# Gated linear attention and a sticky top-1 MoE on one core: next states scaled on ScalarE, and matmuls of zeros moved inside the output product

## The chip, the cores and the metric

The kernel runs on one core of a Trainium2 chip. Times are device microseconds of one execution; the number that counts is the median over the timed runs. Engines are named as in the profile: PE (matrix products), DVE (VectorE), ACT (ScalarE), POOL (GpSimd), SP (SyncE, which here only issues DMAs). PEld is PE's loading of weights.

## The reference, cut to what matters

Four sequences, eight heads, 768 tokens, head dimension 48. Each head keeps a 48x48 state that decays per row and takes in k times v; then each token of 384 numbers goes to one of eight experts:

```python
for t in range(S):
    state = alpha[:, :, t, :, None] * state + np.einsum('bhd,bhe->bhde', k[:, :, t], v[:, :, t])
    y[:, :, t] = np.einsum('bhd,bhde->bhe', q[:, :, t], state)
...
fresh_e = int(np.argmax(logits[b, s]))
e = fresh_e if s == 0 or local_gate[b, s] < 0.5 else prev_e
h = np.maximum(x[b, s] @ w1[e], 0.0)        # 384 -> 1024
out[b, s] = p[e] * (h @ w2[e])              # 1024 -> 384, p: softmax of the logits
```

A token may keep the expert of the token before it (`prev_e`), so the choice runs in order through each sequence.

## The kernel before, in words

**Blocks.** The attention is done in 24 blocks of 128 tokens (two chunks of 64, `C`): block i is chunk pair i // 4 of sequence i % 4, so four blocks, a group, advance all four sequences by 128 tokens, and the state that block i leaves is the start of block i + 4. Four heads lie beside each other twice (partitions 0 to 47 and 64 to 111). The pieces of a block, with the lines of the functions:

- `load_a`, `load_x`, `load_v` (299 to 313): SP issues the loads of decays, of k and q, and of v. `first_v` (315) copies the first 64 rows of v on ACT, beside a half of zeros, so that one product can serve both chunks.
- `scan1` (319): DVE runs products of the decays (`A`) and their reciprocal, POOL scales q by `A`. `scan2` (336): DVE runs the backward scan `sf`, POOL scales k. `one_a` (332): a small POOL memset in the decays that these scans need.
- `kt` (344): PE transposes k into the PSUM tile `kp`, ACT copies it out as `kk`.
- `pm` (353): PE makes the products of k and q (`pe`), DVE masks them into `pq`.
- `um` (369): PE makes the updates `up` from `kk` and v; DVE adds them to the start state and so makes `st`.
- `copies` (390): two ACT copies bring `st` into the operand `sb`. `state` (395): DVE scales the end state by the decay of the block and writes it as the start of block i + 4.
- `ym` (403): PE makes y into one PSUM tile, first the products of `pq` with v (the value products, 32 in the trace), then those of q with `sb` (the state products, 16). ACT copies y out as `XR` and issues the DMA of `XR` to DRAM (`xd`).
- `xt` (421): PE transposes `XR` into `xp`, ACT copies that to `xx` for the router.

PSUM tiles have one buffer for each tag. `kp` and `xp` have the same tag, `tr`: `xp` of block i - 2 comes after `kp` of block i and is written only when `kk` of block i has been copied out.

**The order.** The engines take their instructions in the order in which the program writes them (`pinned`, line 660 on). In pass i of the loop: `scan2(i+1)`, `kt(i)`, `copies(i-1)`, `state(i-1)`, `pm(i)`, other, `scan1(i+2)`, loads of block i + 3, `xt(i-2)`, `ym(i-1)`, `first_v(i+1)`, a weight step in passes 5 to 11, other, `um(i)`, other.

**Other** (622) fills in work that isn't the block's. It takes one step of the routing generator of a group (`route`, 432: about three steps a block, each up to its next `yield`). Then, until group 2 has been routed, it issues two matmuls of zeros (`dense(DN)`, 293: 128x256, into a tile `h2` that nobody reads). After that it takes pieces of the first expert jobs (`early`, 562: gather rows, transpose them, eight gemm1 steps of nine products, gemm2) for the rows that groups 0 to 2 have given to experts 0 and 1. Expert products are fp32 split in two parts: the high half is cast by ACT, the low half is a difference on DVE, and three products replace one. **A weight step** makes the halves of a slice of expert 0's weights: ACT casts at once, and the low half is put off (`later`, 288) until the next other, that is, ahead of `um` and so ahead of `st` on DVE.

After block 23 and the last routing, the remaining jobs run one after the other, PE full.

Every instruction goes through a helper on line 81, so the profile shows L81 for all of them, and tiles tell them apart. The lines that set the two orders that the change touches:

```python
            if i < NB:
                kt(i)
            if 0 < i <= NB:
                copies(i - 1)
                state(i - 1)
```

Of the kernel before, what the change touches and what calls it, by code (L numbers as in the profile page):

```python
# [42 lines left out]
EARLY = (0, 1)  # L43
NEXT = 2

DN0 = 32
DN = 2
HL = ("h", "h", "up", "pe")
YL = ("yp", "y")
RT = "rt"  # L50
# [16 lines left out]
def gla_moe(ctx, tc, akq, vw, vn, wg, w1, w2, cst, tok, out):  # L67
# [45 lines left out]
    def cc(k, p0=0, p1=128):  # L113
        a, b = _off[k]
        return cs[p0:p1, a:b]
# [140 lines left out]
    with ExitStack() as ac, ExitStack() as aa:  # L256
# [15 lines left out]
            VTs.append(vt)  # L272
        for j in range(2):
            sb = ap.tile([R, 2, 2, CW], F32, bufs=1, name=f"sb{j}")
            g_.memset(sb[0:64], 0.0)
            g_.memset(sb[64:112, :, 1, :], 0.0)
            SBs.append(sb)
            oh = ap.tile([128, E, G + 1], F32, bufs=1, name=f"oh{j}")
            g_.memset(oh, 0.0)
            OHs.append(oh)  # L280

        st = {"c": c0}
        sts = [ap.tile([R, 3, HP, D], F32, tag="st", bufs=G + 1, name=f"st_{i}") for i in range(G)]
# [9 lines left out]
        def dense(n):  # L293
            for _ in range(n):
                t_.matmul(h2[:, 0, 0:C1], lhsT=dz[:, 0:128], rhs=dz[:, 0:C1], start=True, stop=True)
# [15 lines left out]
        def load_v(i):  # L311
            at = i % G * NBB + i // G
            y_.dma_start(VTs[i % NP][:, 1, :], vn[:, at * DM:(at + 1) * DM])

        def first_v(i):
            vt = VTs[i % NP]
            s_.copy(vt[0:64, 0, :], vt[0:64, 1, :])

        def scan1(i):

            d = blk[i]
            x, a = d["x"], d["a"]
            A = ap.tile([R, SW], F32, tag="A", bufs=3, name=f"A_{i}")
            v_.tensor_tensor_scan(A, a[:, 0:SW], z1, 0.0, ALU.mult, ALU.add)
            d["end"] = A[:, 2 * C + 1:SW:2 * (C + 1)]
            v_.reciprocal(z2[0:R, 2 * C + 1:SW:2 * (C + 1)], d["end"])
            q2 = x[:, BW:].rearrange("p (s t) -> p s t", t=C)
            g_.tensor_tensor(q2, q2, A.rearrange("p (s t) -> p s t", t=C + 1)[:, :, 1:], ALU.mult)
            d["k"] = x[:, 0:BW].rearrange("p (h t) -> p h t", h=HP)
            d["q"] = x[:, BW:2 * BW].rearrange("p (h t) -> p h t", h=HP)  # L330

        def one_a(i):
            a = blk[i]["a"]
# [61 lines left out]
        def state(i):  # L395
            d = blk[i]
            if i + G < NB:
                sn = ap.tile([R, 3, HP, D], F32, tag="st", bufs=G + 1, name=f"st_{i + G}")
                v_.scalar_tensor_tensor(sn[:, 0], d["s3"][:, 2], 1.0 / SEED,
                                        d["end"].unsqueeze(2).broadcast_to([R, HP, D]), ALU.mult, ALU.mult)  # L400
                st["S", i % G] = sn

        def ym(i):
            d = blk[i]
            vt, pq = d["vt"][:, 1, :], d["pq"]
            sb = d["sb"].rearrange("p c e (h d) -> p c e h d", h=HP)
            yw = pp.tile([128, 512], F32, tag="y", name=f"y_{i}")
            for h in range(H):
                for c in range(2):
                    r = slice(c * C, (c + 1) * C)  # L410
                    t_.matmul(yw[r, h * D:(h + 1) * D], lhsT=pq[r, h % 2, h // 2, :], rhs=vt[r, h * D:(h + 1) * D],
                              start=(h == 0), stop=False, skip_group_check=True)
            for hp in range(HP):
                for c in range(2):
                    t_.matmul(yw[c * C:(c + 1) * C, 2 * hp * D:2 * (hp + 1) * D], lhsT=d["q"][:, hp, c * C:(c + 1) * C],
                              rhs=sb[:, c, :, hp, :], start=False, stop=(hp == HP - 1), skip_group_check=True)
            d["XR"] = ap.tile([128, DM], F32, tag="XR", bufs=3, name=f"XR_{i}")
            s_.copy(d["XR"], yw[:, 0:DM])
            a_.dma_start(xd[1 + i * 128:1 + (i + 1) * 128], d["XR"])
# [12 lines left out]
        def route(g):  # L432
# [4 lines left out]
            def rt(shape, nm, dt=F32, bufs=2):  # L437
                return ap.tile(shape, dt, tag=nm, bufs=bufs, name=f"{nm}_{g}")
# [27 lines left out]
            v_.scalar_tensor_tensor(m2, kr[:, 1, :, 0], 16.0, m2, ALU.mult, ALU.add)  # L466
            v_.tensor_tensor(kr[:, 0], ge, m2.unsqueeze(2).broadcast_to([128, n, 8]), ALU.is_equal)
            yield
            yield

            rp = pp.tile([8 * n, 2, 128], F32, tag=RT, name=f"rp_{g}")
            for j in range(2):
# [23 lines left out]
            v_.tensor_reduce(se, ex, AX.X, ALU.add)  # L496
            v_.tensor_scalar_add(se, se, 1e-9)
            v_.reciprocal(se, se)
            yield
            v_.tensor_tensor(ex, ex, ob, ALU.mult)  # L500
            pn = rt([128, n], "pn")
            v_.tensor_reduce(pn, ex, AX.X, ALU.add)
            v_.tensor_tensor(pl[:, :, 0], pn, se, ALU.mult)
            yield
            pw = pp.tile([128, E, n + 1], F32, tag=RT, name=f"pw_{g}")
            t_.matmul(pw.rearrange("p e b -> p (e b)"), lhsT=one, rhs=oi.rearrange("p e b -> p (e b)"),
                      start=True, stop=False)
            t_.matmul(pw[:, :, 0:n], lhsT=trif, rhs=o4, start=False, stop=True)
            yield
            ps = rt([128, E, n + 1], "ps")  # L510
            v_.tensor_tensor(ps, pw, st["c"].unsqueeze(2).broadcast_to([128, E, n + 1]), ALU.add)
            po = rt([128, n, 8], "po")
# [20 lines left out]
            (v_ if end else g_).tensor_tensor(vo, oa.unsqueeze(2).broadcast_to([128, n, 3, E * NS]),  # L533
                                              pl.unsqueeze(3).broadcast_to([128, n, 3, E * NS]), ALU.mult)
            on = ap.tile([128, n, TS], F32, bufs=1, tag="on", name=f"on_{g}")
            if end:
                v_.tensor_tensor(on, iob.unsqueeze(1).broadcast_to([128, n, TS]),
                                 rr.unsqueeze(2).broadcast_to([128, n, TS]), ALU.is_equal)
            else:
                for j in range(n):  # L540
                    s_.activation(on[:, j], iob, AF.Abs, bias=rr[:, j:j + 1], scale=-1.0)
                    s_.activation(on[:, j], on[:, j], AF.Relu, bias=one[:, 0:1], scale=-float(TS))
                    if j < n - 1:
                        yield
            yield

            lp = pp.tile([128, 3 * E * NS], F32, tag=RT, name=f"lp_{g}")
# [14 lines left out]
        def early():  # L562
# [7 lines left out]
                j.load_list(0)  # L570
            for _ in jobs[0].gather():
                yield False
            for _ in range(4):
                yield False
            for _ in jobs[0].trans():
                yield True
            for n, j in enumerate(jobs):
# [41 lines left out]

        last, EW, steps = [], {}, []  # L620

        def other(pieces=True):

            flush()
            for r in list(steps):
                if next(r, 0) == 0:
                    steps.remove(r)
            if work[0] is None:
                if DN:
                    dense(DN)  # L630
            else:
                if last and drained[0]:
                    last[0].ht, last[0].yt = HL, YL
                for done in work[0] if pieces else ():
                    if done or steps or not drained[0]:
                        break

        work, drained = [None], [False]
        for i in range(3):
# [3 lines left out]
            if i == 0:  # L643
                nc.scalar.dma_start(cs, cst)
                nc.scalar.dma_start(tk, tok)
                nc.scalar.dma_start(wgs, wg[:, :, 0:32])
        g_.memset(one, 1.0)
        g_.memset(m5, 1.0)
        g_.memset(m5[:, :, 0], 0.0)
        for e in range(E):  # L650
            g_.memset(c0[:, e:e + 1], float(e * RS - 1))
            g_.memset(c1[:, e:e + 1], float(e * RS - 1 + (C1 if e in EARLY else 0)))
        g_.tensor_copy(trif, cc("tri"))
        g_.memset(trif[0:64, 64:128], 1.0)
        g_.memset(trif[64:128, 0:64], 0.0)
        nc.scalar.dma_start(xd[0:1], z2[127:128, 0:DM])
        first_v(0)
        pinned[0] = True
        dense(DN0)
        made = [  # L660
            lambda: g_.memset(fill, 0.0),
            lambda: g_.tensor_copy(fill.bitcast(I32)[:, 1:2], tk[0:SL, 2 * NB:]),
            lambda: g_.memset(acc, 0.0),
# [10 lines left out]
                                     tk[:, 0:2 * NB].rearrange("p (b j t) -> p t j b", b=G, t=2)[:, 0],  # L674
                                     -float(SENT), None, ALU.add),
            lambda: g_.tensor_copy(vals[:, :, 2], tk[:, 1:2 * NB:2]),
        ]
        one_a(0)
        scan1(0)
        scan2(0)  # L680
        one_a(1)
        scan1(1)
        wsteps = iter(())
        for i in range(NB + 2):
            if i + 2 < NB:
                one_a(i + 2)
            if i + 1 < NB:
                scan2(i + 1)
            flush()
            if i < NB:  # L690
                kt(i)
            if 0 < i <= NB:
                copies(i - 1)
                state(i - 1)
            if i < NB:
                pm(i)
            if i > NB:
                drained[0] = True
            for _ in range(min(3, len(made))):
                made.pop(0)()  # L700
            other(i >= NB)
            if i + 2 < NB:
                scan1(i + 2)
            if i + 3 < NB:
                load_a(i + 3)
                load_x(i + 3)
            if i > 1:
                xt(i - 2)
                if (i - 1) % G == 0:
                    steps.append(route((i - 2) // G))  # L710
            if 0 < i <= NB:
                ym(i - 1)
                if i + 2 < NB:
                    load_v(i + 2)
            if i + 1 < NB:
                first_v(i + 1)
            if i == W0:
                begin(EARLY[0], v_)
                wsteps = EW[EARLY[0]].steps()
            elif i > W0 + 2:  # L720
                next(wsteps, None)
            if i == T1:
                begin(EARLY[1], v_)
            other()
            if i < NB:
                um(i)
            other()
# [213 lines left out]
```

## Time and profile before

| what | value |
| --- | --- |
| median of 3 runs | 488.33 us (485.93 to 488.93) |
| profiled execution | 484.0 us, span 482.2 us |
| PE busy | 437.9 us (91%) |
| DVE busy | 257.3 us (53%) |
| ACT busy | 194.1 us (40%) |
| POOL busy | 186.7 us (39%) |
| mean granted clock | 0.961 |
| matmuls of zeros | 142, 35.0 us |
| blocks (first scan to the last `st`) | 6.34 to 169.10 us |

The shares are means over three stages. Up to about 150 us the blocks run and DVE is nearly always busy; from there to 201 us the last blocks, the last routing and the first expert share the engines; from 260 to 470 us PE is busy all the time with expert products (210.00 of 210.00 us). In a row of the order of time stand start and length, engine, line, operation, output and inputs with shapes, the number of merged instructions, and in brackets how long the engine had been idle and what ended that. The start of one `st` and the next gives a block's time.

### The profile page before, as it was taken

To read this page: it belongs to the slowest core of one execution; us is meant where nothing else is said; L and a number is where in the kernel's file an instruction comes from. 1 tells how busy PE (TensorE), PEld (TensorE's weight loads), DVE (VectorE), ACT (ScalarE), POOL (GpSimd) and SP (SyncE) were. 2 spreads that over 40 slices of the span, in tenths; PEclk is the share of its full clock that TensorE was granted. 3 is DMA by queue.
4 is the path that set the end of the run, shared out by engine and by line. 5 is a ranking of instruction groups with operands and counts; after the bars stand their busy time and mean duration, and the time that the engine had idled before them with its cause. 6 is when DMAs were issued, how large, how long until landed. Compare 5 with 4: busy or idle time off the path is not lost.

```text
span 482.2 us, 10873 instructions
## 1 busy us (share of the span) xinstructions
PE 437.9 (91%) x4443; PEld 391.5 (81%) x4443; DVE 257.3 (53%) x485; ACT 194.1 (40%) x390; POOL 186.7 (39%) x207
## 2 busy tenths in 40 slices
PE   5999898999997978698989999999999999999990
PEld 5777776878875877597878998998989989989990
DVE  4778999898997235722274445244254252342310
ACT  1345656565756436321354324335144233242210
POOL 6654326364556000261053642724732503504201
PEclk9799999999998899888899999999999999999997
DMA  8789767596661102660075554444351542531100
GB/s 217 199 260 252 222 187 201 164 292 167 189 208 50 51 17 71 180 186 27 1 224 188 134 181 138 124 131 123 114 175 57 158 130 65 174 98 39 50 3 27
DMA packets 26710, 66.01 MB, mean 137 GB/s; under 512 B 4384, under 2 KB 10677, under 8 KB 26658
## 3 DMA queue, kind: packets, MB, share of 16 engines
q1 hardware_dynamic: 18672, 49.65, 36.3%
q0 software_dynamic: 3840, 10.62, 6.9%
q10 hardware_dynamic: 4146, 5.03, 3.1%
q8 instruction: 35, 0.57, 0.5%
q14 instruction: 17, 0.14, 0.1%
HBM read 55.84 MB, written 10.62 MB: 138 GB/s over the span
## 4 chain that ended last, share of the span: by engine, by line
PE 53%; issue 11%; DVE 9%; ACT 3%; POOL 2%; POOLq 0%; DVEq 0%; ACTq 0%
PE h L81 24%; PE yp L81 20%; PE y L81 3%; PE tp L81 2%; DVE A L81 2%; POOL out L81 1%; PE up L81 1%; DVE st L81 1%; DVE sf L81 1%; DVE pq L81 1%; ACT hh L81 1%; POOL w1l_0b L81 1%; PE pe L81 1%; DVE xl L81 1%; PE lp L81 1%
## 5 line engine op out<-in xcount | busy, mean ns | idle before, releaser
L81 DVE SCALAR_TENSOR_TENSOR hl<-h,hh 128x480 fp32r<-128x480 f32 (+2 forms) x80 | 43.9, 556 | 77.2 <-ACT hh L81 76.9
L81 ACT ACTIVATE hh<-h 128x480 fp32r<-128x480 f32 (+2 forms) x80 | 38.7, 490 | 82.4 <-PE h L81 82.3
L81 POOL DMA_INDIRECT out<-yo,idx x32 | 32.5, 1017 | 80.5 <-DVE yo L81 78.0
L81 POOL DMA_INDIRECT xg<-xd,idx x32 | 32.6, 1018 | 61.0 <-PE tp L81 52.9
L81 DVE TENSOR_SCALAR yo<-yp,acc 128x384 f32<-128x384 f32 (+1 forms) x32 | 19.6, 616 | 61.1 <-PE yp L81 61.0
L81 POOL TENSOR_TENSOR x<-x,sf 112x512 f32<-112x512 f32 x24 | 29.0, 1209 | 42.5 <-DVE sf L81 42.5
L81 POOL TENSOR_TENSOR x<-x,A 112x512 f32<-112x512 f32 x24 | 31.8, 1327 | 29.0 <-DVE A L81 6.6
L81 DVE TENSOR_TENSOR_SCAN A<-a,z 112x520 f32<-112x520 f32 x24 | 34.5, 1437 | 5.6 <-POOL a L81 5.6
L81 PE MATMUL h<-dz 128*128 128x256 f32 x142 | 35.0, 354 | 2.1 <-DVE z L81 2.1
L81 DVE TENSOR_TENSOR_SCAN sf<-a,z 112x520 f32<-112x520 f32 x24 | 33.8, 1408 | 0.1
L81 ACT COPY sb<-st 48x384 f32<-48x384 f32 x48 | 24.5, 510 | 11.5 <-DVE st L81 10.9
L81 PEld LDWEIGHTS h<-dz 128*128 128x128 f32 x142 | 23.8, 224 | 6.5 <-DVE z L81 2.1
L81 PEld LDWEIGHTS y<-vt,pq 64*64 64x64 f32 x768 | 24.9, 138 | 4.0 <-issue 3.8
L81 PE MATMUL y<-vt,pq 64*64 64x48 f32 x768 | 27.9, 224 | 0.0
L81 PE MATMUL y<-sb,x 112*64 112x96 f32 x384 | 21.8, 258 | 4.3 <-ACT sb L81 4.2
L81 PE MATMUL up<-vt,kk 128*48 128x96 f32 (+1 forms) x384 | 23.1, 267 | 0.0
L81 PEld LDWEIGHTS y<-sb,x 112*64 112x64 f32 x384 | 17.2, 140 | 6.2 <-ACT sb L81 5.2
L81 PEld LDWEIGHTS up<-vt,kk 128*48 128x48 f32 (+1 forms) x384 | 18.3, 140 | 3.4 <-issue 1.0
L81 ACT COPY kk<-kp 128x448 f32<-128x448 f32 x24 | 12.8, 531 | 20.7 <-PE kp L81 20.6
L81 PE MATMUL h<-xh,w1h_1a 128*128 128x256 f32 (+1 forms) x48 | 16.4, 342 | 3.9 <-DVE hl L81 2.7
L81 ACT COPY XR<-y 128x384 f32<-128x384 f32 x24 | 11.5, 479 | 20.1 <-PE y L81 20.1
L81 ACT CAST xh<-tp 128x384 fp32r<-128x384 f32 (+1 forms) x32 | 14.0, 462 | 13.9 <-PE tp L81 13.6
(247 smaller groups left out, 1234.8 us busy)
## 6 DMA issues: line engine op xcount, KB each, us to landing
x<-akq SPq DMA_DIRECT2D x24, 448.0 KB, 5.6
a<-akq SPq DMA_DIRECT2D x24, 227.9 KB, 4.5
vt<-vn SPq DMA_DIRECT2D x24, 192.0 KB, 2.7
xd<-XR ACTq DMA_DIRECT2D x24, 192.0 KB, 4.8
rw_0a<-w SPq DMA_DIRECT2D x3, 512.0 KB, 4.9
rw_0a<-w SPq DMA_DIRECT2D x4, 384.0 KB, 4.2
rw_1a<-w SPq DMA_DIRECT2D x3, 512.0 KB, 5.9
rw_1a<-w SPq DMA_DIRECT2D x4, 384.0 KB, 3.5
```

The source lines that it names most:

```text
L81: r = f(*a, **k)
```

## The change

1. `DN` goes from 2 to 0: the six matmuls of zeros of each block go. `DY` = 3 of them are put into `ym`, between the value and the state products, until group 2 has been routed. The 32 at the start stay.
2. `state`: the multiplication on DVE becomes four ACT activations (112x48, a scale for each partition) for every block up to 19; the scale `dec` is made by a small POOL operation in `scan1`.
3. `kt(i)` comes after `copies(i-1)` and `state(i-1)`.
4. `first_v` goes; a second DMA on SP brings the 64 rows.
5. In block 0 the scaling of q comes after that of k on POOL. Memsets of POOL from the start go into the list `made`, which is worked off five at a time instead of three; `c0` is made on DVE.
6. `route`: one empty step goes; the product of `ex` with the one-hot `ob` goes to POOL (`eo`), and `pn` behind the products `pw`; `on` is one DVE comparison instead of eight ACT activations over four steps. `early` waits two steps instead of four. A group's routing has 10 steps, before 15 (the last group's has fewer).

```diff
+DY = 3
 DN0 = 32
-DN = 2
+DN = 0
...
             y_.dma_start(VTs[i % NP][:, 1, :], vn[:, at * DM:(at + 1) * DM])
-
-        def first_v(i):
-            vt = VTs[i % NP]
-            s_.copy(vt[0:64, 0, :], vt[0:64, 1, :])
+            y_.dma_start(VTs[i % NP][0:64, 0, :], vn[0:64, at * DM:(at + 1) * DM])
...
+            if i + G < NB:
+                d["dec"] = ap.tile([R, HP], F32, tag="dec", bufs=4, name=f"dec_{i}")
+                g_.tensor_scalar(d["dec"], d["end"], 1.0 / SEED, None, ALU.mult)
...
                 sn = ap.tile([R, 3, HP, D], F32, tag="st", bufs=G + 1, name=f"st_{i + G}")
-                v_.scalar_tensor_tensor(sn[:, 0], d["s3"][:, 2], 1.0 / SEED,
-                                        d["end"].unsqueeze(2).broadcast_to([R, HP, D]), ALU.mult, ALU.mult)
+                for hp in range(HP):
+                    s_.activation(sn[:, 0, hp], d["s3"][:, 2, hp], AF.Copy, scale=d["dec"][:, hp:hp + 1])
...
+            if work[0] is None:
+                dense(DY)
             for hp in range(HP):
                 for c in range(2):
                     t_.matmul(yw[c * C:(c + 1) * C, 2 * hp * D:2 * (hp + 1) * D], lhsT=d["q"][:, hp, c * C:(c + 1) * C],
...
-            if end:
-                v_.tensor_tensor(on, iob.unsqueeze(1).broadcast_to([128, n, TS]),
-                                 rr.unsqueeze(2).broadcast_to([128, n, TS]), ALU.is_equal)
-            else:
-                for j in range(n):
-                    s_.activation(on[:, j], iob, AF.Abs, bias=rr[:, j:j + 1], scale=-1.0)
-                    s_.activation(on[:, j], on[:, j], AF.Relu, bias=one[:, 0:1], scale=-float(TS))
-                    if j < n - 1:
-                        yield
+            v_.tensor_tensor(on, iob.unsqueeze(1).broadcast_to([128, n, TS]),
+                                              rr.unsqueeze(2).broadcast_to([128, n, TS]), ALU.is_equal)
...
-            for _ in range(4):
-                yield False
+            yield False
+            yield False
...
             flush()
-            if i < NB:
-                kt(i)
             if 0 < i <= NB:
                 copies(i - 1)
                 state(i - 1)
             if i < NB:
+                kt(i)
+            if i < NB:
                 pm(i)
             if i > NB:
                 drained[0] = True
-            for _ in range(min(3, len(made))):
+            for _ in range(min(5, len(made))):
                 made.pop(0)()
```

What it moves on the engines, at three places. First ACT in pass 15 of the blocks, before and now; numbers behind names are blocks and buffers.

```order
L81 COPY kk_15_1843<-kp_15_1838 128x448
L81 COPY sb0_104<-st_14_1379 48x2x192 x2
L81 COPY xx_3_1772<-xp_13_1880 128x384
L81 COPY XR_14_1910<-y_14_1885 128x384
L81 DMA xd_83<-XR_14_1910 128x384
L81 COPY vt1_100<-vt1_100 64x384
```

```order
L82 COPY sb0_104<-st_14_1378 48x2x192 x2
L82 ACTIVATE st_18_1848<-st_14_1378,dec_14_1541 112x48 x4
L82 COPY kk_15_1858<-kp_15_1853 128x448
L82 COPY oh0_107<-rb_2_1879 128x8x4
L82 COPY xx_3_1785<-xp_13_1892 128x384
L82 COPY XR_14_1925<-y_14_1897 128x384
L82 DMA xd_83<-XR_14_1925 128x384
```

The copy `kk` has moved behind the two copies of `st` of the block before and behind four new activations; the copy of v is gone.

Second, PE at the same place, before and now (`rb` is a routing step, `dz` the zeros):

```order
L81 MATMUL kp_15_1838<-cs_66,x_15_1520 128x112 x4
L81 MATMUL pe_15_1849<-x_15_1520 64x64 x16
L81 MATMUL h2_118<-dz_93 128x256 x2
L81 MATMUL xp_13_1880<-cs_66,XR_13_1803 128x128 x3
L81 MATMUL y_14_1885<-vt2_102,pq_14_1746 64x48 x16
L81 MATMUL y_14_1885<-sb0_104,x_14_1410 64x96 x8
L81 MATMUL rb_2_1915<-cs_66,em_2_1868 128x32
L81 MATMUL h2_118<-dz_93 128x256 x2
```

```order
L82 MATMUL kp_15_1853<-cs_66,x_15_1546 128x112 x4
L82 MATMUL pe_15_1860<-x_15_1546 64x64 x16
L82 MATMUL rb_2_1879<-cs_66,em_2_1840 128x32
L82 MATMUL xp_13_1892<-cs_66,XR_13_1819 128x128 x3
L82 MATMUL y_14_1897<-vt2_102,pq_14_1761 64x48 x16
L82 MATMUL h2_114<-dz_93 128x256 x3
L82 MATMUL y_14_1897<-sb0_104,x_14_1420 64x96 x8
```

The zeros stand now between the two parts of y, three instead of two at a time, and none stand ahead of `xp`, `up` and `kp`.

Third, PE where the first expert's gemm1 begins (`h` from `xh`): before behind the products of block 22's pass, now in pass 20.

```order
L81 MATMUL y_21_2672<-vt0_98,pq_21_2534 64x48 x16
L81 MATMUL y_21_2672<-sb1_109,x_21_2230 64x96 x8
L81 MATMUL lp_3_2701<-vo_3_2536,on_3_2538 128x96 x4
L81 MATMUL tp_0_0_1_2707<-cs_66,xg_0_0_1_2377 128x128 x3
...
L81 MATMUL rp_4_2723<-cs_66,kr_4_2654 32x128 x2
L81 MATMUL h2_118<-xh_0_0_2613,w1h_0a_0_730 128x256
```

```order
L82 MATMUL kp_20_2434<-cs_66,x_20_2120 128x112 x4
L82 MATMUL pe_20_2441<-x_20_2120 64x64 x16
L82 MATMUL xp_18_2484<-cs_66,XR_18_2383 128x128 x3
L82 MATMUL y_19_2489<-vt1_100,pq_19_2340 64x48 x16
L82 MATMUL y_19_2489<-sb1_108,x_19_2014 64x96 x8
L82 MATMUL h2_114<-xh_0_0_2396,w1h_0a_0_734 128x256
```

The first gemm1 step has moved two passes ahead and stands between the state products of y of block 19 and `up` of block 20.

More of the change, by code (lines that the diff above doesn't have):

```diff
@@ L274, in gla_moe @@
             sb = ap.tile([R, 2, 2, CW], F32, bufs=1, name=f"sb{j}")
-            g_.memset(sb[0:64], 0.0)
-            g_.memset(sb[64:112, :, 1, :], 0.0)
+            if j == 0:
+                g_.memset(sb[0:64], 0.0)
+                g_.memset(sb[64:112, :, 1, :], 0.0)
             SBs.append(sb)
-            oh = ap.tile([128, E, G + 1], F32, bufs=1, name=f"oh{j}")
-            g_.memset(oh, 0.0)
-            OHs.append(oh)
+            OHs.append(ap.tile([128, E, G + 1], F32, bufs=1, name=f"oh{j}"))
         st = {"c": c0}
@@ L326, in scan1, with scale_q @@
             v_.reciprocal(z2[0:R, 2 * C + 1:SW:2 * (C + 1)], d["end"])
-            q2 = x[:, BW:].rearrange("p (s t) -> p s t", t=C)
-            g_.tensor_tensor(q2, q2, A.rearrange("p (s t) -> p s t", t=C + 1)[:, :, 1:], ALU.mult)
+            d["A"] = A
+            if i + G < NB:
+                d["dec"] = ap.tile([R, HP], F32, tag="dec", bufs=4, name=f"dec_{i}")
+                g_.tensor_scalar(d["dec"], d["end"], 1.0 / SEED, None, ALU.mult)
+            if i:
+                scale_q(i)
             d["k"] = x[:, 0:BW].rearrange("p (h t) -> p h t", h=HP)
             d["q"] = x[:, BW:2 * BW].rearrange("p (h t) -> p h t", h=HP)
+        def scale_q(i):
+            q2 = blk[i]["x"][:, BW:].rearrange("p (s t) -> p s t", t=C)
+            g_.tensor_tensor(q2, q2, blk[i].pop("A").rearrange("p (s t) -> p s t", t=C + 1)[:, :, 1:], ALU.mult)
         def one_a(i):
@@ L498, in route @@
             v_.reciprocal(se, se)
[L499 to L503, printed above, removed]
+            eo = rt([128, n, 8], "eo")
+            g_.tensor_tensor(eo, ex, ob, ALU.mult)
             yield
@@ L509, in route @@
             yield
+            pn = rt([128, n], "pn")
+            v_.tensor_reduce(pn, eo, AX.X, ALU.add)
+            v_.tensor_tensor(pl[:, :, 0], pn, se, ALU.mult)
             ps = rt([128, E, n + 1], "ps")
@@ L535, in route @@
             on = ap.tile([128, n, TS], F32, bufs=1, tag="on", name=f"on_{g}")
-            if end:
-                v_.tensor_tensor(on, iob.unsqueeze(1).broadcast_to([128, n, TS]),
-                                 rr.unsqueeze(2).broadcast_to([128, n, TS]), ALU.is_equal)
-            else:
-                for j in range(n):
-                    s_.activation(on[:, j], iob, AF.Abs, bias=rr[:, j:j + 1], scale=-1.0)
-                    s_.activation(on[:, j], on[:, j], AF.Relu, bias=one[:, 0:1], scale=-float(TS))
-                    if j < n - 1:
-                        yield
+            v_.tensor_tensor(on, iob.unsqueeze(1).broadcast_to([128, n, TS]),
+                                              rr.unsqueeze(2).broadcast_to([128, n, TS]), ALU.is_equal)
             yield
@@ L620, in gla_moe, with other @@
         last, EW, steps = [], {}, []
-        def other(pieces=True):
+        def other(pieces=True, dn=DN):
             flush()
@@ L628, in other @@
             if work[0] is None:
-                if DN:
-                    dense(DN)
+                dense(dn)
             else:
@@ L646, in gla_moe @@
                 nc.scalar.dma_start(wgs, wg[:, :, 0:32])
[L647 to L655, printed above, removed]
         nc.scalar.dma_start(xd[0:1], z2[127:128, 0:DM])
-        first_v(0)
         pinned[0] = True
@@ L660, in gla_moe @@
         made = [
+            lambda: g_.memset(SBs[1][0:64], 0.0),
+            lambda: g_.memset(SBs[1][64:112, :, 1, :], 0.0),
+            lambda: g_.memset(one, 1.0),
+            lambda: g_.memset(OHs[0], 0.0),
+            lambda: g_.memset(OHs[1], 0.0),
+            lambda: g_.memset(m5, 1.0),
+            lambda: g_.memset(m5[:, :, 0], 0.0),
+            lambda: g_.tensor_copy(trif, cc("tri")),
+            lambda: g_.memset(trif[0:64, 64:128], 1.0),
+            lambda: g_.memset(trif[64:128, 0:64], 0.0),
             lambda: g_.memset(fill, 0.0),
@@ L676, in gla_moe @@
             lambda: g_.tensor_copy(vals[:, :, 2], tk[:, 1:2 * NB:2]),
+            lambda: v_.tensor_scalar(c0, ioa[:, :, 0], WH, float(TS), ALU.subtract, ALU.mult),
+            lambda: v_.tensor_scalar(c0, c0, -1.0, None, ALU.add),
+            lambda: g_.tensor_copy(c1, c0),
+        ] + [
+            lambda e=e: g_.memset(c1[:, e:e + 1], float(e * RS - 1 + C1)) for e in EARLY
         ]
@@ L680, in gla_moe @@
         scan2(0)
+        scale_q(0)
         one_a(1)
@@ L714, in gla_moe @@
                     load_v(i + 2)
-            if i + 1 < NB:
-                first_v(i + 1)
             if i == W0:
```

## Prediction

> **What bounds the kernel now.** I read the stretches, then the chain of waits, then the rows of single blocks in order of time. From 95 to 115 us (columns: length, then busy time of PE, PEld, DVE, ACT, POOL, granted clock, DMA share, GB/s) two engines are full at once:
>
> ```profile
> 95.00:115.00 20.00, 19.27 (x391) 16.08 (x392) 18.33 (x41) 12.50 (x32) 11.25 (x12) 1.00 0.81 249
> ```
>
> The chain of waits runs there through DVE or through PE. Four of its PE pieces, start and length:
>
> ```profile
> 112.65 0.43 PE h L81 x2
> 113.08 0.81 PE up L81 x16
> ...
> 114.33 0.39 PE kp L81 x4
> 114.72 0.62 PE pe L81 x32
> ```
>
> The pieces of `h` are matmuls of zeros; there are three pairs in a block, 1.3 us of PE. So some of what fills PE can go. The block times come from the additions that make a block's state (`st`), first and last of each stage:
>
> ```profile
> 18.72 0.56 DVE L81 TENSOR_TENSOR st<-up,st 112x384 f32<-112x384 f32 x1 [1.27 <-POOL a L81]
> ...
> 24.31 0.56 DVE L81 TENSOR_TENSOR st<-up,st 112x384 f32<-112x384 f32 x1 [1.27 <-POOL a L81]
> ...
> 40.78 0.53 DVE L81 TENSOR_TENSOR st<-up,st 112x384 f32<-112x384 f32 x1
> ...
> 90.35 0.55 DVE L81 TENSOR_TENSOR st<-up,st 112x384 f32<-112x384 f32 x1
> ...
> 119.70 0.56 DVE L81 TENSOR_TENSOR st<-up,st 112x384 f32<-112x384 f32 x1 [0.29 <-PE up L81]
> ...
> 168.18 0.88 PE L81 MATMUL up<-vt,kk 128*48 128x96 f32 x16
> ...
> 169.10 0.36 DVE L81 TENSOR_TENSOR st<-up,st 112x192 f32<-112x192 f32 x1 [3.58 <-PE up L81]
> ```
>
> They are blocks 0, 1, 4, 11, 16 and 23: 5.59 us for the first block, 7.08 for each of the seven with a step of expert weights (40.78 to 90.35), 5.87 from 11 to 16, 7.06 from 16 to 23. All 23 average 6.54. After block 23 PE works off the experts.
>
> **The change: a ring through kk.** PE's transposes `xp` of block i-2 and `kp` of block i share one PSUM buffer, so `xp` waits until ACT has copied `kk` of block i out of it. Before, `kk` stood ahead of everything else of its block on ACT. In the changed order it stands behind the two `sb` copies and the four new activations, and these wait for `st` of block i-1. Behind `xp` on PE stand y of block i-1, then `up` of block i, which makes `st` of block i. So each block runs once round: st, sb twice, four activations, kk, xp, value products of y, three matmuls of zeros, state products, up, st. Rows of its pieces, from several blocks:
>
> ```profile
> 36.56 0.56 DVE L81 TENSOR_TENSOR st<-up,st 112x384 f32<-112x384 f32 x1 [1.54 <-POOL st L81]
> ...
> 37.15 1.03 ACT L81 COPY sb<-st 48x384 f32<-48x384 f32 x2 [1.39 <-DVE st L81]
> ...
> 38.09 0.47 ACT L81 COPY xx<-xp 128x384 f32<-128x384 f32 x1
> ...
> 42.49 1.14 PE L81 MATMUL y<-vt,pq 64*64 64x48 f32 x32
> ...
> 43.56 0.88 PE L81 MATMUL y<-sb,x 112*64 112x96 f32 x16
> ...
> 44.37 0.86 PE L81 MATMUL lg<-xx,wgs 128*32 128x128 f32 x24
> ...
> 53.70 0.22 ACT L81 ACTIVATE ex<-ex 128x32 f32<-128x32 f32 x1
> 53.84 0.51 ACT L81 COPY kk<-kp 128x448 f32<-128x448 f32 x1
> ...
> 54.40 0.55 PE L81 MATMUL xp<-cs,XR 128*128 128x128 f32 x3
> 54.87 1.14 PE L81 MATMUL y<-vt,pq 64*64 64x48 f32 x32
> ...
> 71.38 0.40 ACT L81 ACTIVATE on<-on,one 128x128 f32<-128x128 f32 x1
> ```
>
> Start to start: st to sb 0.59 (36.56 to 37.15); the sb pair 0.94 (to 38.09); kk to xp 0.56 (53.84 to 54.40); xp to y 0.47; value to state products 1.07 (42.49 to 43.56); three zeros 0.65 (by the 0.43 of a pair); state products 0.81 (to 44.37); up to st 0.92 (168.18 to 169.10). The activations of 112x48 are not in the trace. The activation of 128x32 let the next instruction start after 0.14, the one of 128x128 was busy 0.40: four cost 0.56 to 1.60. A row of 48 elements is nearest to the first; I take 0.16 each, 0.64. The ring is 0.59 + 0.94 + 0.64 + 0.56 + 0.47 + 1.07 + 0.65 + 0.81 + 0.92 = 6.65 us. In one block of four the 24 routing matmuls (0.8) stand between y and up, in others smaller ones: 6.9 on average.
>
> In this order `sb` has landed before `xp` starts, so the zeros between y's two parts wait for nothing there and lengthen the ring by their 0.65. The three pairs that are removed had filled PE; their 1.3 us come off no ring.
>
> **Weight steps.** In the seven blocks with one, `st` stands on DVE behind the low half of a weight, which waits for ACT's cast, and that stands on ACT behind the copy `XR` of y. The ring leaves PE after the state products and goes this way:
>
> ```profile
> 38.23 0.88 PE L81 MATMUL y<-sb,x 112*64 112x96 f32 x16 [0.59 <-ACT sb L81]
> ...
> 39.16 0.48 ACT L81 COPY XR<-y 128x384 f32<-128x384 f32 x1 [0.60 <-PE y L81]
> ...
> 40.03 0.51 ACT L81 COPY vt<-vt 64x384 f32<-64x384 f32 x1 [0.40 <-DMA vt<-vn]
> ...
> 45.78 1.04 ACT L81 CAST w1h_0a<-rw_0a 128x1024 fp32r<-128x1024 f32 x1
> ...
> 46.85 1.23 DVE L81 TENSOR_TENSOR w1l_0a<-rw_0a,w1h_0a 128x1024 fp32r<-128x1024 f32 x1 [1.18 <-ACT w1h_0a L81]
> ...
> 48.00 0.55 DVE L81 TENSOR_TENSOR st<-up,st 112x384 f32<-112x384 f32 x1
> ...
> 88.61 0.83 ACT L81 CAST w2h_0a<-rw_0a 128x768 fp32r<-128x768 f32 x1
> ...
> 89.47 0.96 DVE L81 TENSOR_TENSOR w2l_0a<-rw_0a,w2h_0a 128x768 fp32r<-128x768 f32 x1 [1.96 <-ACT w2h_0a L81]
> ```
>
> Up to the state products it is 4.92 (the first seven terms). Then XR 0.93 later (38.23 to 39.16), the next on ACT 0.87 (past the DMA issue, to 40.03, where the vt copy goes and the cast moves up), cast to low half 1.07, to st 1.15: 8.94 for three blocks. With the narrower casts 0.86 and 0.88: 8.46 for four. Together 60.7, and 1.3 more for route operations behind the low half: 62.0, against 49.57.
>
> **What costs nothing on this ring.** The 20 multiplications off DVE: DVE, with 0.9 of its time taken before, gets a longer block. The vt copies become 24 DMAs of 96 KB on SP: SP issues them ahead of need, and at 249 GB/s (first row) the block of 5.9 us moves 1.5 MB, so 6% more. If they came late, value products would wait; I see no such wait in the rows and allow 0 to 3 us. POOL's products for the routing and `dec` lie in a POOL half idle (11.25 of 20). On PE, `kt` moves past nothing. The memsets that leave the start bring the first scan forward, which waited for one behind them:
>
> ```profile
> 6.34 1.24 DVE L81 TENSOR_TENSOR_SCAN A<-a,z 112x520 f32<-112x520 f32 x1 [4.23 <-POOL a L81]
> ```
>
> Of the 4.23 us I take 0.7 as gained, with 0 and 2.5 as bounds, since the load of `a` must land too.
>
> **The tail.** Routing takes fewer steps, so the first expert's products start two blocks earlier: eight gemm1 steps lie in blocks 20 to 23, where before two did:
>
> ```profile
> 169.84 0.38 PE L81 MATMUL h<-xh,w1h_0a 128*128 128x256 f32 x1 [0.78 <-DVE hl L81]
> ...
> 172.11 0.39 PE L81 MATMUL h<-xh,w1h_0a 128*128 128x256 f32 x1 [0.93 <-DVE hl L81]
> ...
> 201.30 0.36 PE L81 MATMUL h<-xh,w1h_1a 128*128 128x256 f32 x1
> ```
>
> A step is 2.27 us (169.84 to 172.11); six leave the stretch between st of block 23 and the next expert's first product, 169.10 to 201.30, 13.6 us. The last group's routing must still pass in it, so I take 10, with 6 to 14 as bounds. What goes into the blocks: one step of nine products in each ring of blocks 20 to 23 (1.2 each), the other outside the ring.
>
> **The sum, clock held.** Block 0 to 4: 5.59 + 3 x 6.65 = 25.5 for 22.1, +3.5. Blocks 4 to 11: +12.4. 11 to 16: 5 x 6.9 = 34.5 for 29.35, +5.1. 16 to 23: 7 x 6.9 + 4 x 1.2 + 1 for the transposes of the gathered tokens = 54.1 for 49.4, +4.7. The start −0.7, the tail −10. Together **+15**.
>
> **The clock.** PE now idles while it waits for kk. Its work in a plain block is 0.39 + 0.62 (kp, pe) + 0.47 + 1.07 + 0.65 + 0.81 + 0.81 = 4.8; the gap is 1.8 us, with a weight step 3.7 to 4.1. The granted clock moved in this trace in steps of 3.41 us:
>
> ```profile
> 55.18:58.59 3.41, 1.91 (x48) 1.56 (x43) 3.41 (x7) 1.87 (x4) 1.21 (x1) 1.00 1.04 317
> 58.59:62.00 3.41, 3.41 (x25) 2.89 (x24) 2.71 (x4) 1.54 (x3) 1.23 (x2) 0.51 0.98 306
> ...
> 191.71:195.12 3.41, 2.04 (x13) 1.70 (x14) 2.03 (x6) 2.03 (x4) 1.05 (x1) 1.00 0.77 251
> ```
>
> PE idled 1.50 us of the first window and the next one ran at 0.51; 1.37 idle, in the third row, left it up (195 on). Cold, the products of y took:
>
> ```profile
> 153.98 1.78 PE L81 MATMUL y<-vt,pq 64*64 64x48 f32 x32
> ...
> 155.69 1.55 PE L81 MATMUL y<-sb,x 112*64 112x96 f32 x16
> ```
>
> That is 0.64 and 0.67 over the warm 1.14 and 0.88, on the ring: 1.3 a block. The seven weight blocks have a gap of over a window, so +9. A 1.8 us gap lies within one window about half the time: of some 11 plain blocks without gemm1 steps half, 1 us each, +5.5, bounds 0 and 14. The Trainium skill, "TensorE: Matmul & The Clock Gate" (section "Why this matters for your kernels"), asks for no idle gap over about 3 us, since one whole idle window drops the clock. By that rule plain blocks would stay warm (a rival below); the row of 58.59 speaks against it, as half a window of idling was enough there.
>
> In all 15 + 9 + 5.5 = +29.6. The profiled execution took 484.0 us (span 482.2, 1.8 around it); it becomes 513.6. The median of the runs is 488.33, 4.3 above the profiled one, so the forecast for the median is **518 us**, slower.
>
> **The rivals.**
> - *Only gaps over a window drop the clock.* Weight blocks go cold, plain ones stay warm: 488.3 + 15 + 9 = 512. For it: the row of 191.71, where 1.37 us idle did nothing, and kp and pe that split the wait in two; against: the row of 58.59. 14%.
> - *The clock stays up in weight blocks too*, because the drops fall on kp and pe, off the ring: 488.3 + 15 = 503. Against: y stands right behind the gap. 9%.
> - *The zeros fill a real wait.* If sb came after the value products, the three matmuls would cover PE's idle time, cost nothing in the 14 rings with them (−9) and keep plain blocks warm (−5.5): 503. For it: before, PE waited 0.59 for sb at 38.23. Against: kk now comes after sb on ACT and releases xp, so sb is always there. 8%.
> - *No ring: DVE and PE set the block* (the other side). If kk cost no wait, plain blocks would fall to what DVE and PE have to do: 5.5, DVE's 18.33 of 20 us less the multiplication, PE's less the 1.3 of zeros. With weight blocks at 7.08 as now, st of block 23 comes at 18.7 + 5.6 + 3 x 5.5 + 49.6 + 5 x 5.5 + 7 x 6.3 = 162, 7 us earlier; with the tail −17: 471. It decides at the mean block: with 10 us off the tail, blocks may be 0.43 longer than 6.54, so up to 6.97 is no loss. Plain rings at 6.9 are just there, and it is the weight blocks' 8.5 to 8.9 that lose; for this rival st to kk must take under 1.3 us where I add up 2.2. 8% faster.
> - *Losses just meet the tail* (weight blocks' ring shorter by the cast going ahead of XR, warm clock): 488, 4%.
> - *Slow activations and a cold clock throughout*: four at 0.40 add 1.0 in 19 rings, 537. The nearest small activation speaks against it. 10%.
>
> My own forecast has 47%. A measurement of this kernel tells about 1% from no change. Faster by over 1%: 0.08; within 1%: 0.04; slower: 0.88. The range 497 to 534 takes in the 503s and most of the slow activations; below it lie the 12% of the fourth and third rival, above it some 7%.
>
> **What would show it.** Right: st of block 23 at 205 to 213 us instead of 169; xp released by ACT kk with PE idle 1.5 us or more in nearly every block; sb done before the value products start, and no wait at the state products; weight blocks at 8.5 us and more, plain at 6.6 to 7.5; the granted clock at 0.5 in several windows between 40 and 110; the first product of the next expert about 22 us after st of block 23. Wrong: blocks under 6.5 us, a PE idle time that ends with sb behind the zeros, or a clock at 1.00 throughout.

## The result

The changed kernel took 545.12 us (median of 4 runs, 543.73 to 546.43) against 488.19: 1.117 times as long, interval 1.113 to 1.122. Slower, as forecast, but far over the range: 518 was said, 497 to 534. Its profiled span is 544.6 us. The stages, from one `st` to another:

| stage | before | now | difference | forecast, clock held |
| --- | --- | --- | --- | --- |
| blocks 0 to 4 | 22.1 | 30.9 | +8.8 | +3.5 |
| 4 to 11 (weight steps) | 49.6 | 79.1 | +29.5 | +12.4 |
| 11 to 16 | 29.4 | 45.7 | +16.3 | +5.1 |
| 16 to 23 | 49.4 | 62.7 | +13.3 | +4.7 |
| `st` 23 to the next expert's first product | 32.2 | 24.2 | −8.0 | −10 |

The rest is the start (+0.2) and the experts behind (+2.2). For the clock the forecast added 14.5 to the sum of its column.

**The ring is there.** The longest waits of the changed kernel have a row that before had not (us in total, times, longest):

```profile
PE xp L82 <- ACT kk L82: 28.2, 19, 3.8
```

Nine of the 19 waits reached 1.5 us, where the forecast had them in nearly every block.

And its chain of waits in the blocks 12 to 14 (start, length, what) is the ring, piece by piece, first warm, then cold:

```profile
138.42 0.57 DVE st L82
...
139.01 0.51 ACT sb L82
...
139.53 0.51 ACT sb L82
140.04 0.91 ACT st L82 x4
140.96 0.42 ACT kk L82
...
141.42 0.55 PE xp L82 x3
141.97 1.06 PE y L82 x32
143.03 0.55 PE h L82 x3
143.59 0.81 PE y L82 x16
144.40 0.79 PE lg L82 x24
145.19 0.82 PE up L82 x16
...
146.04 0.57 DVE st L82
...
149.04 0.90 PE xp L82 x3
149.94 1.88 PE y L82 x32
151.82 0.94 PE h L82 x3
152.76 1.48 PE y L82 x16
154.24 0.54 PE rp L82 x2
154.78 1.34 PE up L82 x16
...
156.14 0.57 DVE st L82
```

The first round took 7.62 us, the second 10.10. On PE the second, at half clock, paid 0.35 more for `xp`, 0.82 for the value products, 0.39 for the zeros, 0.67 for the state products, 0.52 for `up`: 2.75 us of cold clock. The clock shows in stretches of one step each (length, busy time of PE, PEld, DVE, ACT, POOL, granted clock, DMA share, GB/s):

```profile
142.23:145.64 3.41, 3.41 (x83) 2.91 (x81) 1.38 (x2) 1.00 (x3) 1.52 (x4) 1.00 1.00 293
145.64:149.05 3.41, 1.64 (x48) 1.25 (x43) 2.98 (x5) 2.54 (x8) 1.18 (x1) 0.99 0.95 271
149.05:152.47 3.42, 3.42 (x38) 2.99 (x38) 2.15 (x7) 0.48 (x1) 1.16 (x2) 0.50 0.06 16
152.47:155.88 3.41, 3.41 (x36) 2.56 (x34) 0.00 (x0) 0.86 (x3) 0.26 (x2) 0.51 0.82 174
155.88:159.29 3.41, 1.70 (x44) 1.26 (x40) 3.15 (x5) 2.43 (x8) 1.00 (x1) 0.99 0.51 178
```

PE waits 1.77 us for `kk` in the second row; the next two are cold though PE is busy all through them, and the fifth has the next wait. Of 43 such stretches from 33 to 180 us 28 were cold (half clock), in the kernel before 3. The same over whole stages, blocks 4 to 11 and 11 to 16 of the changed kernel:

```profile
49.82:128.91 79.09, 61.77 (x812) 51.13 (x812) 41.59 (x78) 31.15 (x80) 19.44 (x33) 0.63 0.48 133
128.91:174.57 45.66, 39.83 (x575) 33.57 (x574) 27.39 (x60) 17.44 (x50) 15.89 (x23) 0.69 0.56 158
```

**A second wait, not forecast.** In the weight blocks PE also stood still at routing products, here at `pw`, in another at `lp`:

```profile
83.82 0.39 PE L82 MATMUL pw<-oi,one 128*128 128x40 f32 x2 [2.60 <-DVE se L82]
...
95.75 0.50 PE L82 MATMUL lp<-vo,on 128*128 128x96 f32 x1 [2.21 <-DVE on L82]
```

### The profile page after: what moved, and what is told of

It is laid out like the page before. It is cut to its first block, busy times and chain, and to the rows that moved or that the text cites. A ratio compares the mean times of both kernels' runs of the same rounds, so it can differ in the third digit from the quotient of the medians.

```text
span 544.6 us, 10817 instructions
## 1 busy us (share of the span) xinstructions
PE 472.3 (87%) x4381; PEld 419.8 (77%) x4381; DVE 249.5 (46%) x466; ACT 187.4 (34%) x406; POOL 188.0 (35%) x220
## 4 chain that ended last, share of the span: by engine, by line
PE 65%; issue 10%; ACT 10%; DVE 6%; POOL 4%; DMA 3%; ACTq 0%; POOLq 0%; DVEq 0%
PE h L82 23%; PE yp L82 19%; PE y L82 11%; ACT sb L82 3%; PE up L82 3%; PE xp L82 3%; ACT st L82 3%; POOL x L82 2%; DVE st L82 2%; PE tp L82 2%; ACT kk L82 1%; PE lp L82 1%; DMA xd<-XR 1%; PE lg L82 1%; POOL out L82 1%
## 5 line engine op out<-in xcount | busy, mean ns | idle before, releaser
L82 POOL DMA_INDIRECT out<-yo,idx x32 | 32.2, 1006 | 74.6 <-DVE yo L82 60.5
L82 PE MATMUL xp<-cs,XR 128*128 128x128 f32 x72 | 16.2, 344 | 28.4 <-ACT kk L82 28.2
L82 PEld LDWEIGHTS y<-vt,pq 64*64 64x64 f32 x768 | 35.0, 184 | 5.3 <-issue 5.3
L82 PE MATMUL y<-vt,pq 64*64 64x48 f32 x768 | 38.4, 269 | 0.0
L82 ACT COPY sb<-st 48x384 f32<-48x384 f32 x48 | 24.5, 510 | 32.4 <-DVE st L82 31.6
L82 DVE TENSOR_TENSOR st<-up,st 112x384 f32<-112x384 f32 (+1 forms) x24 | 12.5, 520 | 50.2 <-PE up L82 44.9
L82 PEld LDWEIGHTS xp<-cs,XR 128*128 128x128 f32 x72 | 9.3, 167 | 31.4 <-ACT kk L82 30.8
L82 PE MATMUL y<-sb,x 112*64 112x96 f32 x384 | 32.2, 337 | 0.0
L82 PEld LDWEIGHTS y<-sb,x 112*64 112x64 f32 x384 | 25.9, 197 | 4.0 <-issue 2.9
L82 PEld LDWEIGHTS up<-vt,kk 128*48 128x48 f32 (+1 forms) x384 | 25.8, 183 | 3.9 <-issue 2.9
L82 PE MATMUL kp<-cs,x 112*128 112x112 f32 x96 | 17.2, 313 | 6.8 <-POOL x L82 5.5
L82 PE MATMUL h<-dz 128*128 128x256 f32 x80 | 20.7, 407 | 2.1 <-DVE z L82 2.1
```

Source lines behind the costliest of these rows:

```text
L82: r = f(*a, **k)
```

## The experiments

They ran on four other chips than the result; there the kernel before took 482.5 to 482.9 us, 1.1 per cent less. Each run is given with its median, its ratio to the kernel before in the same job, and the interval of that; expectations in us are best compared through the ratio, times 488.

**The place of kk alone, both ways.** `kt_first` is the changed kernel with

```diff
+            if i < NB:
+                kt(i)
             if 0 < i <= NB:
                 copies(i - 1)
                 state(i - 1)
-            if i < NB:
-                kt(i)
```

> The changed kernel with kt(i) back ahead of copies and state, all else as changed. Ring theory (kk's late place on ACT holds xp through the shared PSUM buffer, the idle gap that this makes drops the clock): no wait of xp for kk over 0.3 us, blocks of 5.5 to 6 us (weight blocks up to 7), granted clock back near 0.95, st of block 23 near 165, about 480 us. Rival (the zeros taken out of the blocks are what lets the clock fall, the order matters little): clock still under 0.75 between 50 and 180 us, blocks over 7 us, over 510 us. Rival (the activations on ACT are the price): 24 x 1 us less than now at most are kept, over 500 us.

503.83 us, 1.042 (1.033 to 1.051). Most of the loss is gone, and the waits of `xp` for `kk` are gone from the list of waits. But 4 per cent stay where 480 us was expected, and the clock is still 0.74 in blocks 4 to 11, so this run alone does not rule out the rivals.

`own_psum` keeps the order and takes away what makes `xp` wait, in blocks 0 to 17:

```diff
-            xp = pp.tile([128, DM], F32, tag="tr", name=f"xp_{i}")
+            xp = pp.tile([128, DM], F32, tag="yp" if i < 18 else "tr", name=f"xp_{i}")
```

> The changed kernel with xp of blocks 0 to 17 in the PSUM buffer of the expert output yp, which is unused then, so that xp no longer waits for kk; order unchanged. Ring theory: kk then holds only up, the round is st, sb, activations, kk, up, st, some 3.9 us, and doesn't bind: 478 to 490 us up to the ring of blocks 20 to 23, clock near 0.95. Rival (zeros): as the changed kernel, 535 to 545. Rival (activations ahead of kk on ACT by themselves): between, 510 to 530.

508.98, 1.050 (1.037 to 1.064), about what `kt_first` gives, but not the 478 to 490 of the ring theory. Through the ratio it is 513, at the low end of the third theory; yet `kt_first` has no activations ahead of `kk` and costs nearly as much. So it is the shared PSUM buffer through which the late `kk` costs, and what is left has another cause. The clock was still 0.77 in blocks 4 to 11, which took 60.9 us, and these waits on PE were left:

```profile
64.17 0.62 PE L82 MATMUL pw<-oi,one 128*128 128x40 f32 x2 [3.01 <-DVE se L82]
...
75.69 0.71 PE L82 MATMUL lp<-vo,on 128*128 128x96 f32 x2 [2.22 <-DVE on L82]
...
138.57 1.82 PE L82 MATMUL lp<-vo,on 128*128 128x96 f32 x8 [4.42 <-POOL a L82]
```

`before_kt_late` is the reverse edit in the kernel before.

> The kernel before with one edit: kt(i) after copies(i-1) and state(i-1). Ring theory: the round is st, sb, kk, xp, y, a pair of zeros, up, st: 5.7 us plus routing, about 8 with a weight step (before 7.1): plain blocks nearly unchanged, weight blocks about 1 us longer, 494 to 502 us. Rival (the activations or the zeros are the price, the place of kk alone is not): 486 to 491 us.

501.80, 1.038 (1.028 to 1.048), through the ratio 507, above the 502 expected: the late `kk` costs also without any other part of the change, 12 us in blocks 4 to 11, at a clock of 0.78, and 3 us in 11 to 16 at a full clock (32.4 for 29.4).

**The zeros.** `fill_old` has `DN = 2` and `DY = 0`, kk late:

> The changed kernel with the zeros as before: a pair in each of the three places of a block, none inside y. kk stays late. Ring theory: the ring stays (warm 6.7 to 7 us plain, 9 with a weight step), two of the pairs fill PE's wait for kk, so the clock holds in plain blocks and drops in weight blocks: 515 to 528 us. Rival (zeros): the clock is back at 0.95 and the time near before plus little, 485 to 500.

528.79, 1.097 (1.088 to 1.107): far from the 485 to 500 of the zeros, and through the ratio (535) above the 528 of the ring. The clock rose to 0.81 in blocks 4 to 11 and 0.87 in 11 to 16, and `xp` still waited 21 us in all for `kk`.

`no_fill` has `DY = 0`:

> The changed kernel without its three matmuls of zeros inside y (no zeros after the start). Ring theory: they wait for nothing there and lengthen the ring by 0.55 warm, 0.94 cold, in 14 rings: 8 to 13 us less, ratio 1.09 to 1.10. Rival (inside y they hold the clock up): no gain or a loss, ratio 1.115 to 1.14.

527.07, 1.094 (1.078 to 1.110). Taking the three zeros out of y gains, so they covered no wait; that the clock then came back to 0.86 in blocks 11 to 16 was not expected.

`gap_fill` puts zeros where PE really waits, ahead of `xp` (the second argument is their number):

```diff
-            other(i >= NB)
+            other(i >= NB, 16 if W0 + 2 < i < 12 else 8)
```

> The changed kernel with zeros also where PE waits for kk (ahead of xp): eight a block, sixteen in the blocks with a weight step, until group 2 is routed. The ring is not longer by them as long as they fit into the wait (1.7 us of eight, 3.4 of sixteen). Clock theory (the price of the ring is mostly the cold clock that its gaps bring, two windows and more for each gap): clock above 0.9 from 25 to 170 us, blocks 6.9 and 9.2 us, ratio 1.04 to 1.06. Length theory (the ring itself is the price): clock up, blocks as now, ratio 1.10 to 1.12.

528.72, 1.096 (1.086 to 1.106), just under the 1.10 of the length theory and far from the other. Blocks did get shorter with the clock, though: it came back to 0.90 in blocks 4 to 11, and a weight block without routing products took 9.13 us, as reckoned for the ring. Others still took 11 to 12.9, with waits of 1.8 to 2.9 us at `rb`, `pw` and `lp`.

**The activations.** `stt` puts the next state back on DVE (`scalar_tensor_tensor` for the four activations):

> The changed kernel with the next state on DVE again, so that kk stands behind the sb copies alone; kk late, routing short, zeros in y. Takes 0.91 us off the ring and off PE's gap, 1.8 to 0.9 in a plain block. Length theory: 19 x 0.9 = 17 us less, ratio 1.08. Clock theory: plain blocks also stay warm (gap under the 1.2 to 1.5 us that dropped the clock), ratio 1.05 to 1.07.

520.27, 1.082 (1.071 to 1.093). The plain blocks 14 to 16 fell to 6.2 us at a clock of 0.90 in their stage; the weight blocks fell too (68.5 us for 4 to 11, after 79.1), but at a clock of 0.75. The ratio is that of the length theory, the clock that of the other; the run tells them apart badly.

**The routing.** By now a second theory stood beside the ring: the shorter routing puts PE's products close behind the DVE and POOL operations that feed them, and since PE works in order, everything stands behind them. `kt_first_route_old` is `kt_first` with `route` and the four waiting steps of `early` as before.

> kt_first with the routing and the start of the first expert as before (15 steps a group, the comparison on ACT, four waiting steps). kt_first left 4 per cent of loss over before, with PE waits of 2.2 to 4.4 us at the routing products pw and lp. Routing theory (the shorter routing puts PE's routing products close behind the DVE and POOL work that they need, PE stands still, the clock falls): those waits shrink below 1.5 us, st of block 23 at 165 to 172, ratio to before 0.99 to 1.01. Rival (without zeros in the three places the clock falls whatever waits): clock under 0.85 from 40 to 140 us, ratio 1.03 to 1.05.

485.87, 1.0075 (1.003 to 1.012, 10 runs). The waits at `pw` and `lp` in the blocks are gone (one of 2.0 us at `rp` is left), and so is the cold clock from block 4 to 16, with no zeros outside y (blocks 4 to 11, then 11 to 16):

```profile
41.72:89.34 47.62, 39.88 (x813) 32.39 (x812) 45.16 (x76) 33.20 (x88) 26.73 (x35) 1.00 0.78 215
89.34:118.08 28.74, 27.22 (x538) 22.35 (x537) 27.35 (x56) 19.49 (x57) 14.23 (x18) 1.00 0.89 256
```

`kt1_route0_fill0` is that with the zeros as before:

> kt_first_route_old with the pairs of zeros as before too: what is left of the change is the next state on ACT, the second DMA for v, and the start. Both theories: ratio 0.99 to 1.00. Against kt_first_route_old it is the effect of the zeros alone: routing theory within 1 per cent of it, zeros theory 3 to 4 per cent faster than it.

488.18, 1.012 (1.004 to 1.020): above the 0.99 to 1.00 of both theories, but within noise of `kt_first_route_old`, as the routing theory has it. Where PE hardly waits, moving these zeros matters neither way.

`before_route_new` has the changed `route` and `early` in the kernel before:

> The kernel before with the changed routing and start of the first expert alone (pairs of zeros as before, kk early). Routing theory: PE waits of 2 us and more at pw and lp, blocks with them 1 to 4 us longer, some of it given back by the tail's 8 us: ratio 1.00 to 1.03. Rival (zeros): the pairs of zeros keep the clock, the blocks stay and the tail gains: 0.98 to 0.99.

505.42, 1.044 (1.039 to 1.050), above both ranges. The tail gained 9 us (23.2 for 32.2), the blocks lost 28, with a clock of 0.75 in 4 to 11 in spite of the pairs of zeros.

`route_old` is the changed kernel with the old routing, kk late:

> The changed kernel with the routing and the start of the first expert as before; kk late, zeros inside y. If the losses of the ring and of the routing add: 1.117 less the 0.04 of kt_first, ratio 1.07 to 1.09. If the ring alone makes the idle gaps and the clock, and the routing costs only when the ring is gone: 1.10 to 1.13 (the tail 8 us longer as well).

553.84, 1.142 (1.136 to 1.148): worse than the changed kernel, outside both expectations. So in the changed kernel as it stands, with its gaps unfilled, the shorter routing gains. The clock of `route_old` was 0.53 in blocks 11 to 16. That the old routing's eight activations, some of which stand on ACT ahead of `sb` and `kk`, lengthen the ring is argued, not shown.

`gap_fill_route_old` adds the zeros ahead of `xp` to it, to see the ring by itself:

> gap_fill (clock mostly up) with the routing as before. Open: whether the 11 to 13 us of the weight blocks with routing products (rb, pw, lp) in gap_fill come from the shorter routing. If so: those blocks fall to 9.2 to 9.8 us, 4 to 11 in 64 to 67 us instead of 71.5, but the tail is 8 longer: ratio 1.09 to 1.10. If any routing does this under the late kk (its activations on ACT stand ahead of kk too): 4 to 11 in 70 us or more, ratio over 1.11.

525.00, 1.086 (1.073 to 1.099), a little better than expected for a routing that is to blame, though the intervals of the two runs overlap. Blocks 4 to 11 here and in `gap_fill`:

```profile
47.88:110.65 62.77, 54.53 (x963) 47.15 (x964) 40.83 (x75) 33.72 (x88) 20.00 (x31) 1.00 0.58 160
```

```profile
47.74:119.23 71.49, 58.57 (x925) 51.19 (x925) 41.89 (x78) 31.18 (x80) 19.54 (x33) 0.90 0.52 144
```

At a full clock the seven weight blocks took 62.8 us, each between 8.6 and 9.1. The shorter routing adds 8.7 to that, with the cold clock that goes with it; in blocks 11 to 16 it is the other way (38.2 for 41.5).

**Can it be had without the price?** `kt1_spaced` is `kt_first` with three `yield`s back, ahead of `rp`, `pw` and `lp`:

> kt_first with one empty step back ahead of each of rp, pw and lp (a group has 13 routing steps, before 15, changed 10); the rest of the routing as changed. Routing theory (PE's routing products stood too close behind the DVE and POOL operations that they need): PE waits at pw and lp under 1.2 us, clock near 0.95, the start of the first expert still somewhat earlier: ratio 0.985 to 1.000. Rival (the work itself, on POOL and DVE instead of ACT, is the price): 1.02 to 1.04 as kt_first.

491.19, 1.018 (1.008 to 1.028): between. `pw` waits no more, `lp` still waits 1.6 us, now for POOL's `vo`. The comparison is made in the same step as `vo`, and `vo` lies on POOL behind the scaling of k. A wait of 3.1 us at `kp` makes block 21 14.7 us long.

`kt1_route0_early2` is `kt_first_route_old` with two waiting steps in `early`:

> kt_first_route_old with only the start of the first expert changed (two waiting steps instead of four): can some of the tail's gain be had without the closer routing products? If the transposes of the gathered rows then only wait for their DMA: ratio 1.008 to 1.02. If the tail gains and PE does not stand still: 0.995 to 1.003.

488.56, 1.012 (1.004 to 1.020): the tail is 4 us shorter, and a wait of 4 us at `kp` in block 21 eats it.

`kt1_stt_route0` has the next state on DVE:

> kt_first_route_old (ratio 1.0075) with the next state on DVE as before: what remains of the change is the second DMA for v, the start and three zeros inside y for the six. If the activations on ACT make the small loss (sb comes late, PE waits 1.6 us for it at 38.9): 0.995 to 1.002. If the second DMA for v does: 1.005 to 1.012.

492.03, 1.022 (1.014 to 1.030), outside both: in its profile block 14 took 13.1 us after a wait of 3.1 at `lt`, and block 11 9.9 after one of 2.3 at `rp` (6.2 and 7.2 in `kt_first_route_old`). Why is open, and so is what makes the 0.75 per cent. No version beat the kernel before.

## Why the prediction was wrong

**Right: direction, mechanism, warm lengths.** The ring runs as written. Warm, the pieces measured against forecast: the `sb` pair 1.03 for 0.94, the four activations 0.92 for 0.64, `kk` to `xp` 0.46 for 0.56, zeros 0.56 for 0.65, the rest within 0.08; with routing products 7.62 for 7.45. An activation came 0.23 us after the one before, for the 0.16 taken, between the two rows that the forecast had:

```profile
L82 ACT ACTIVATE st<-st,dec x80: 317/319/332, 20.5 to 201.7; 112x48 f32<-112x48 f32 x80
```

(Busy time: smallest, median, largest in ns.) For the seven weight blocks 62.0 was said, and `gap_fill_route_old`, with the old routing, measured 62.8 at a full clock; in four of the seven `xp` still waited 0.5 to 2.0 us for `kk` behind the zeros, so there at least the zeros did not set the length. The zeros in y were taken as length without use, which `no_fill` bears out. The tail gained 8.0 for 10. (A slip: the 12 per cent below the range belong to the fourth and fifth rival, not to "the fourth and third", as the prediction has it.)

**Wrong: the step on the clock.** It charged 1.3 us to each weight block and 1 us to half of 11 plain ones, 14.5 in all, as if a drop lasted for the value and state products of one round. In the changed kernel a drop lasted one to seven stretches of 3.41 us, mostly two, and most rounds had cold ones in them: 28 of 43 stretches were cold, and the cold round shown above paid 2.75, on all its PE pieces. The prediction had the two rows for it: 1.5 us idle was enough, and PE's gap was put at 1.8 to 4.1. It then took a gap for a chance of one half and the price for half a round. `gap_fill`, which takes away most of the cold and leaves the ring, was 16 us faster to block 16 (1.3, 7.6 and 7.5 in the three stages), and still had 9 cold stretches of the 43. From block 0 to 16 the clock was down for 104 us in the changed kernel and for 29 in `gap_fill`; at the same rate all of it would be worth some 23 us. That is an estimate from these two profiles alone, and `gap_fill` changed the zeros too.

**Wrong: the routing as a gain alone.** The sum counted the tail of the shorter routing and no price in the blocks. The step looked at what the routing issues and not at what stands behind it: PE takes its products in order, and an empty step is the time that DVE and POOL need. Alone it costs 4.4 per cent (`before_route_new`). Under the late kk, with the gaps filled, it added 12.1 us from block 0 to 23: 8.7 in blocks 4 to 11 and 7.5 in 16 to 20 (37.0 for 29.5), less 3.3 in 11 to 16 (`gap_fill` against `gap_fill_route_old`). With the gaps unfilled it was a gain (`route_old`), so in the changed kernel itself a net price of the routing is not shown.

**The rivals.** The nearest, slow activations and a cold clock throughout, said 537 and had 10 per cent; its cold clock came, its activations of 0.40 each did not. That only gaps of a whole stretch count, as the Trainium skill has it ("TensorE: Matmul & The Clock Gate", section "Why this matters for your kernels"), doesn't hold here: 1.77 us in one stretch dropped the clock for two. The other side, no ring and lighter PE and DVE, was made to run: `kt_first_route_old` has no ring and 47.6 us where 49.6 were; as a whole it is 0.75 per cent slower. With the zeros put back it was no slower beyond noise (`kt1_route0_fill0`), so what they had cost PE bound nothing.

**What adds up, and what stays open.** One way through the profiles, from block 0 to 23: the sum with the clock held said 176.1 us; `gap_fill_route_old` took 190.8, `gap_fill` 202.9 (the shorter routing, 12.1 more), the changed kernel 218.4 (a colder clock, 15.4 more). The first of these differences, 14.7, still holds 29 us at half clock. Another way would divide the loss otherwise, since clock, ring and routing change each other: the ring's part is 13.4 per cent of the time before with the old routing (`route_old` against `kt_first_route_old`), 7.5 with the new one (the result against `kt_first`).

## What to carry to other kernels

When an instruction is moved behind a wait, look for what shares a buffer with its output: here one copy held up another block's transposes, and everything in order behind them. Price an idle gap of PE by how long the clock stays down after it and by all PE work on the ring in that time, not by the gap. An empty step in a hand-made order may be the room that a slower engine needs; before it is taken out, see which in-order engine then waits.

## What the runs showed of the hardware

The profiles show the granted clock in stretches of 3.41 us, at full or at half, and how long PE idles in a stretch goes with what the next one gets, but not sharply. In all seventeen profiles, from 20 us on, the clock fell after every stretch with more than 1.85 us of PE idle in it and after none with less than 1.16. Of the 121 stretches in between 76 were followed by a drop; why the others were not is open. Here 1.75 us idle left the clock up (`gap_fill_route_old`), and 1.16 dropped it (`fill_old`):

```profile
74.69:78.10 3.41, 1.66 (x14) 1.46 (x13) 3.34 (x9) 2.26 (x7) 0.45 (x1) 1.00 0.94 300
78.10:81.51 3.41, 3.26 (x57) 2.78 (x58) 2.49 (x6) 0.81 (x3) 1.60 (x3) 1.00 0.12 33
```

```profile
50.67:54.09 3.42, 2.26 (x53) 1.67 (x53) 3.42 (x4) 2.60 (x8) 1.25 (x3) 1.00 0.81 257
54.09:57.50 3.41, 3.41 (x60) 3.05 (x60) 0.41 (x2) 0.71 (x2) 1.41 (x3) 0.50 0.24 63
```

It came back only after a stretch with at most 0.56 us idle, and a busy PE was no assurance: where PE was busy all through, the clock was down for one stretch 26 times, for two 24 times, for three 10 times, and once for eight, in `before_kt_late` after a wait of 2.40 us:

```profile
60.03:63.44 3.41, 1.01 (x17) 0.63 (x9) 3.41 (x6) 1.46 (x4) 0.73 (x1) 1.00 0.99 350
63.44:90.75 27.31, 27.31 (x316) 22.75 (x315) 15.56 (x33) 11.85 (x26) 8.25 (x10) 0.50 0.50 140
```

So one wait can cost far more than its own length. And no zeros outside y were needed to keep the clock up: in `kt_first_route_old` PE was busy 39.88 of 47.62 us from block 4 to 11, in many short gaps, at a clock of 1.00.
